# Three x loads sent one pair sooner, statistics rounded in the aggregation, the first tile in halves, the last group in two parts: a transformer block on one core

## Chip, cores and metric

The kernel runs on 1 core of one Trainium2 chip. The metric is the device time of one execution in microseconds (us). The time is the profiled span plus about 2.2 us. Before the change the median was 1081.53 us of 3 runs (1080.9 to 1082.35).

## The reference, cut to what matters

```python
h  = x + attention(layernorm(x))        # x: 2048 x 1024, 32 heads of 32, one shared K and V head
h2 = h + glu(layernorm(h))              # gate and up 1024 x 3584, down 3584 x 1024
# attention: q = x@wq; k = x@wk; v = x@wv; softmax(q k^T / sqrt(32)) v; then @ wo
# glu: (sigmoid(x@w_gate) * (x@w_up)) @ w_down
```

## The kernel before

The rows of x are 16 tiles of 128. The layer norm of tiles 0 and 1 is transposed on TensorE, that of tiles 2 to 15 by transposing transfers. At the very start TensorE runs dummy matmuls whose results nobody uses. K and V are made for two tiles at a time. Then come 512 score groups: each has 8 small row-packed matmuls on TensorE (several of them at once, on different rows of the array) and two exponentials of 128 x 1024 on ScalarE. Between them TensorE does P*V (the exponentials times V, packed by columns), q, the output projection and as much of the feed-forward part as fits; the rest of the feed-forward part stands at the end.

No order is written by hand. A list scheduler with guessed durations builds one list per engine, and the lists are then emitted with semaphores. A moved dependence therefore moves other instructions too, and the tuple `KNOBS` (one entry per eight score groups) steers the order in the middle.

```python
def op(self, eng, fn, deps=(), order=(), occ=60.0, lat=None, prio=5, key=None, nbytes=0): ...
    # (cut) "pe" goes into its list at once; the others wait in a heap until their deps have an end,
    # and the smallest (prio, seq) that is ready goes first
# ... (cut)
def load_x(ts, deps=()):
    sl = slice(ts[0] * P, (ts[-1] + 1) * P)
    o = dma(lambda: SP.dma_start(x_sb[:, ts[0]:ts[-1] + 1, :], xf[sl, :].rearrange("(a p) n -> p a n", p=P)),
            f"x{ts[0]}", P * D * 2 * len(ts), deps, prio=1 if ts[0] > 5 else 0)
# ... (cut)
def stats(ph, ts, srcs, deps, prio, small=None):
    # ... two bn_stats a and b for each tile (cut)
        c = pl.op("dve", lambda k=k, t=t: DVE.bn_aggr(mv[:, ph, t, :], st[:, k, :, :]), [a, b], prio=prio_s, ...)
    d = pl.op("dve", lambda: DVE.tensor_copy(out=mvb[:, ph, sl, :], in_=mv[:, ph, sl, :]), cs, prio=prio_s, ...)  # to bf16
    e = pl.op("dve", lambda: DVE.tensor_copy(out=mvr[:, ph, sl, :], in_=mvb[:, ph, sl, :]), [d], prio=prio_s, ...)
    # ... (cut)
for ts in [[0], [1]] + [[t, t + 1] for t in range(2, NT, 2)]:
    sv = stats(0, ts, [x_sb[:, t, :] for t in ts], [[x_ld[t]] for t in ts], ...)
    # ... centre and scale each tile on VectorE: xnorm[t] (cut)
    if 1 < ts[-1] < NT - 6:
        load_x([ts[-1] + 5, ts[-1] + 6], [xnorm[ts[-1]]])
# ... (cut)
exps[u] = pl.op("act", lambda slot=slot, pb=pb: ACT.activation(
    out=pslot(slot).rearrange("p (a b) -> p a b", a=2), in_=S_ps[:, pb:pb + 2, :],
    func=ACTF.Exp, scale=SCALE), [last] + free, prio=3, **t_act(1024))
# ... (cut)
def mk_D(t, dc):                       # down projection of a tile: 512 of 1024 columns, 28 matmuls
    def after(b, last):
        sl = slice(dc * 512, (dc + 1) * 512)
        e = pl.op("dve", lambda: DVE.scalar_tensor_tensor(
            out=h_sb[:, t % 4, sl], in0=F_ps[:, b, :], scalar=0.5, in1=h_sb[:, t % 4, sl],
            op0=ALU.mult, op1=ALU.add), [last], prio=2, **t_dve(512))
        out_dma[(t, dc)] = dma(lambda: SP.dma_start(of[t * P:(t + 1) * P, sl], h_sb[:, t % 4, sl]), ...)
```

The softmax here doesn't subtract the row's maximum and nothing guards it: scores larger than these inputs give would overflow.

## Time and profile before

| What | Before |
|---|---|
| median of the first 3 runs | 1081.53 us |
| the profiled run, time and span | 1082.78 and 1080.5 us, mean granted clock 0.998 (1 is full speed) |
| TensorE, ScalarE, VectorE busy | 97, 93, 84% |
| last exponential to last matmul | some 62 us, TensorE alone |

One row of the costliest groups is ScalarE's exponentials: count, busy us and mean ns of one, then the idle time before them and what ended it.

```profile
L693 ACT ACTIVATE Pr<-S_ps 128x1024 bf16<-128x1024 f32 x1024 | 969.2, 1179 | 4.7 <-PE S_ps L401 4.5
```

The timeline has 16 of them back to back in 14.97 us, from the first start to the last end. From one start to the next the median of the 984 between 60 and 1012 us is 0.904 us, so 1024 of them need some 926 us of a 1080 us program. A record lasts 1.179 us in the mean, so those of neighbours overlap, and a wait of up to some 0.27 us between two of them leaves no idle time in the profile; this will matter below. The Trainium skill, "ScalarE: Activation LUTs", section "What ACT_TABLE_LOAD costs", gives 186 + 0.833 N ns for such an instruction, of which about 93 ns overlap when they stand back to back: 946 ns for N = 1024, near to the 904 that the trace shows.

### The profile page before, as it was taken

The numbers are of one execution on the slowest core, as the hardware profiler recorded it, in microseconds if no ns is written. First come the engines' busy times: TensorE is split into PE (matmuls) and PEld (weight loads), VectorE is DVE, ScalarE is ACT, GpSimd is POOL, SyncE is SP. The second block draws the span as 40 slices with busy tenths as digits, with TensorE's granted clock in tenths as the row PEclk, the third lists the DMA queues.
The fourth block names the chain that finished last, engine by engine and source line by source line (L and its number), as shares of the span: only waits on it lengthen the run. The fifth ranks groups of instructions, "written<-read, shape, count | busy, mean of one in ns | idle before, by whom it ended". The sixth has DMA issues, their size and how long they took to land.

```text
span 1080.5 us, 31405 instructions
## 1 busy us (share of the span) xinstructions
PE 1045.8 (97%) x12803; PEld 483.2 (45%) x12972; DVE 902.7 (84%) x1750; ACT 1007.9 (93%) x1172; POOL 28.4 (3%) x58
## 2 busy tenths in 40 slices
PE   9999999999999999999999999999999999999998
PEld 6664444444444444444444444444444444444443
DVE  8789989898988889898888889898898989898721
ACT  6899999999999999999999999999999999999610
POOL 2100000000000000000000000000000000000000
PEclk9999999999999999999999999999999999999999
DMA  9997799927969597939659697987969596876994
GB/s 223 177 300 236 184 290 258 280 66 217 243 174 243 148 277 186 288 85 288 159 142 223 165 280 139 258 201 179 236 151 274 120 279 165 229 201 167 281 269 109
DMA packets 309359, 226.60 MB, mean 210 GB/s; under 512 B 121824, under 2 KB 300512, under 8 KB 309216
## 3 DMA queue, kind: packets, MB, share of 16 engines
q1 hardware_dynamic: 307136, 224.46, 81.3%
q8 instruction: 102, 1.67, 0.7%
q10 hardware_dynamic: 2080, 0.13, 0.1%
q14 instruction: 41, 0.34, 0.1%
HBM read 194.12 MB, written 7.86 MB: 187 GB/s over the span
## 4 chain that ended last, share of the span: by engine, by line
PE 77%; ACT 11%; DVE 5%; issue 5%; DMA 2%; SPq 0%; POOL 0%; DVEq 0%; ACTq 0%
PE F_ps L401 64%; PE S_ps L401 13%; ACT Pr L693 9%; DVE Ts L727 2%; DMA ring<-in_A_x_dram 1%; ACT tnh L968 1%; DVE st L338 1%; DVE st L340 1%; DMA zone<-ring 1%; DVE Rc L786 0%; DVE ring L385 0%; DVE hst L972 0%; DVE hact L287 0%; DVE Ts L734 0%; DVE ring L378 0%
## 5 line engine op out<-in xcount | busy, mean ns | idle before, releaser
L693 ACT ACTIVATE Pr<-S_ps 128x1024 bf16<-128x1024 f32 x1024 | 969.2, 1179 | 4.7 <-PE S_ps L401 4.5
L727 DVE TENSOR_TENSOR Ts<-Ts,Pr 128x1024 bf16<-128x1024 bf16 x736 | 482.5, 677 | 33.6 <-ACT Pr L693 31.7
L401 PE MATMUL F_ps<-ring,hnT 128*128 128x512 bf16 (+1 forms) x2005 | 411.8, 380 | 13.1 <-issue 9.6
L401 PEld LDWEIGHTS F_ps<-ring,hnT 128*128 128x128 bf16 (+1 forms) x2089 | 153.3, 97 | 192.3 <-issue 47.3
L401 PE MATMUL F_ps<-zone,hact 128*128 128x512 bf16 (+1 forms) x1153 | 212.1, 380 | 9.0 <-issue 8.2
L401 PE MATMUL S_ps<-QTb,kT 32*128 32x256 bf16 x4096 | 208.8, 273 | 1.1
L401 PEld LDWEIGHTS S_ps<-QTb,kT 32*128 32x128 bf16 x4096 | 64.1, 92 | 209.1 <-ACT Pr L693 143.5
L401 PE MATMUL F_ps<-Pr,Vb 128*32 128x256 bf16 x4096 | 135.3, 274 | 0.3 <-issue 0.3
L968 ACT ACTIVATE tnh<-F_ps 128x512 f32<-128x512 f32 x112 | 83.0, 742 | 43.1 <-PE F_ps L401 43.0
L401 PEld LDWEIGHTS F_ps<-zone,hact 128*128 128x128 bf16 (+1 forms) x1214 | 80.0, 97 | 92.7 <-issue 22.7
L727 DVE TENSOR_TENSOR Ts<-Pr 128x1024 bf16<-128x1024 bf16 x128 | 87.3, 684 | 39.9 <-ACT Pr L693 39.8
L972 DVE SCALAR_TENSOR_TENSOR hst<-tnh,F_ps 128x512 bf16<-128x512 f32 x112 | 76.6, 684 | 43.9 <-PE F_ps L401 40.8
L401 PEld LDWEIGHTS F_ps<-Pr,Vb 128*32 128x32 bf16 x4096 | 97.6, 96 | 30.2 <-issue 17.6
L401 PE MATMUL F_ps<-zone 128*128 128x256 bf16 (+5 forms) x639 | 74.9, 271 | 4.7 <-DMA zone<-ring 2.4
L401 PE MATMUL F_ps<-wo_sb,OT 128*128 128x512 bf16 (+1 forms) x289 | 61.5, 380 | 1.8 <-issue 1.4
L401 PEld LDWEIGHTS F_ps<-zone 128*128 128x128 bf16 (+1 forms) x646 | 43.6, 98 | 26.9 <-issue 7.6
L734 DVE TENSOR_TENSOR Ts<-Ts 128x1024 bf16<-128x1024 bf16 x64 | 44.0, 688 | 1.3
L1002 DVE SCALAR_TENSOR_TENSOR h_sb<-F_ps,h_sb 128x512 bf16<-128x512 f32 x32 | 21.8, 682 | 22.3 <-PE F_ps L401 22.1
L352 POOL TENSOR_SCALAR zb<-mvb 128x1 bf16<-128x1 bf16 (+1 forms) x25 | 10.3, 411 | 997.9 <-DVE mvb L348 997.9
L401 PEld LDWEIGHTS F_ps<-wo_sb,OT 128*128 128x128 bf16 (+1 forms) x304 | 22.4, 97 | 28.0 <-issue 7.0
L771 DVE COPY Oc<-F_ps 128x256 f32<-128x256 f32 x60 | 25.2, 420 | 7.4 <-PE F_ps L401 6.6
L776 DVE TENSOR_TENSOR Oc<-F_ps,Oc 128x256 f32<-128x256 f32 x60 | 25.4, 423 | 4.8 <-PE F_ps L401 3.2
(60 smaller groups left out, 333.2 us busy)
## 6 DMA issues: line engine op xcount, KB each, us to landing
ring<-in_B_w_gate_dram SPq DMA_DIRECT2D x314, 256.0 KB, 4.3
ring<-in_B_w_up_dram SPq DMA_DIRECT2D x310, 256.0 KB, 4.6
zone<-in_B_w_down_dram SPq DMA_DIRECT2D x28, 256.0 KB, 4.0
h_sb<-in_A_x_dram SPq DMA_DIRECT2D x16, 256.0 KB, 4.8
out_dram<-h_sb SPq DMA_DIRECT2D x32, 128.0 KB, 3.0
ring<-in_A_x_dram SPq DMA_DIRECT2D x7, 512.0 KB, 5.4
QTb<-q_scratch SPq DMA_DIRECT2D x14, 256.0 KB, 4.8
Pr<-in_B_w_up_dram SPq DMA_DIRECT2D x14, 256.0 KB, 4.4
```

The lines of the kernel that those rows point to most:

```text
L338: a = pl.op("dve", lambda k=k, src=src: DVE.bn_stats(st[:, k, 0, :], src[:, 0:512]), dep, prio=prio, occ=590, lat=756, order=[st_user.get(k)])
L340: b = pl.op("dve", lambda k=k, src=src: DVE.bn_stats(st[:, k, 1, :], src[:, 512:1024]), dep, prio=prio, occ=590, lat=756, order=[st_user.g ...
L352: f = pl.op("pool", lambda: POOL.tensor_scalar(out=zb[:, ph, sl].unsqueeze(2), in0=mvb[:, ph, sl, 1:2], scalar1=LN_EPS_BF16, scalar2=None, ...
L401: fn = lambda: PE.matmul(o, lhsT=l, rhs=r, start=start, stop=stop, **kw)
L693: exps[u] = pl.op("act", lambda slot=slot, pb=pb: ACT.activation(out=pslot(slot).rearrange("p (a b) -> p a b", a=2), in_=S_ps[:, pb:pb + 2 ...
L727: o = pl.op("dve", lambda T=T, a=a, b=b: DVE.tensor_tensor(out=T, in0=a, in1=b, op=ALU.add), deps, prio=4, **t_dve(1024, 1.92))
L734: merge_ev[G] = pl.op("dve", lambda T4=T4: DVE.tensor_tensor(out=T4[:, :, 0, :], in0=T4[:, :, 0, :], in1=T4[:, :, 1, :], op=ALU.add), [sum ...
L771: oc_ev[G] = pl.op("dve", lambda: DVE.tensor_copy(out=Oc[:, :], in_=O), [last, o_ev.get(G - 1)], prio=0, **t_dve(256))
L776: a = pl.op("dve", lambda: DVE.tensor_tensor(out=Oc[:, :], in0=O, in1=Ob, op=ALU.add), [last, oc_ev[G], o_ev.get(G - 1)], prio=0, **t_dve( ...
L968: tanh_of[n] = pl.op("act", lambda: ACT.activation(out=tnh[:, n % 2, :], in_=F_ps[:, b, :], func=ACTF.Tanh, scale=0.5), [last, tn_user.get ...
L972: e = pl.op("dve", lambda: DVE.scalar_tensor_tensor(out=hst[:, n % NST, :], in0=tnh[:, n % 2, :], scalar=1.0, in1=F_ps[:, b, :], op0=ALU.a ...
L1002: e = pl.op("dve", lambda: DVE.scalar_tensor_tensor(out=h_sb[:, t % 4, sl], in0=F_ps[:, b, :], scalar=0.5, in1=h_sb[:, t % 4, sl], op0=ALU ...
```

## The change

The intent: x arrives before VectorE asks for it, so that TensorE does not run dry near 43 us; the rounding copy of the statistics goes, as the aggregation writes bf16 itself; the first tile starts on its first half; the last sum and store are half as long. The settings of the scheduler were searched again for the new start. Cut: the values of `KNOBS`, a rule that may give an Oc copy (the result of P*V taken out of PSUM) to ScalarE (it never does in this program), and the use of the last new field, which may put the feed-forward sum earlier in VectorE's list.

```diff
-XT = 1000.0
+XT = 1300.0                              # the scheduler's guess for a transposing transfer
-    KNOBS = [(4, 6, 0, 0, 2), ... 65 entries ]
+    KNOBS = [(4, 7, 0, 2, 1, 0, 1), ... 65 entries, all retuned, two more fields ]
-        load_x([0])
+        x0_ld = [dma(lambda hf=hf: SP.dma_start(x_sb[:, 0, hf * 512:(hf + 1) * 512], xf[0:P, hf * 512:(hf + 1) * 512]),
+                     f"x0{hf}", P * D, (), prio=0) for hf in range(2)]
+        x_ld[0] = x0_ld[1]
...
-                c = pl.op("dve", lambda k=k, t=t: DVE.bn_aggr(mv[:, ph, t, :], st[:, k, :, :]), [a, b], prio=prio_s,
+                c = pl.op("dve", lambda k=k, t=t: DVE.bn_aggr(mvb[:, ph, t, :], st[:, k, :, :]), [a, b], prio=prio_s,
...
-            d = pl.op("dve", lambda: DVE.tensor_copy(out=mvb[:, ph, sl, :], in_=mv[:, ph, sl, :]), cs, prio=prio_s,
-                      occ=66, lat=240)
...
+                elif t == 0:
+                    for hf in range(2):
+                        xnorm[hf - 1] = pl.op("dve", lambda xh=xt[:, hf * 512:(hf + 1) * 512], sc=sc: DVE.tensor_scalar(
+                            out=xh, in0=xh, scalar1=sc, scalar2=None, op0=ALU.mult), [cen, sv[1]], prio=-1, occ=200, lat=370)
...
-            if 1 < ts[-1] < NT - 6:
-                load_x([ts[-1] + 5, ts[-1] + 6], [xnorm[ts[-1]]])
+            for k in {3: [8, 10], 5: [12], 7: [14]}.get(ts[-1], []):
+                load_x([k, k + 1], [xnorm[ts[-1]]])
...
-                    for dc in range(2):
-                        queues["D"].append(mk_D(t, dc))
+                    for a in [(0,), (1,)] if t < NT - 1 else [(0,), (1, 0, 256), (1, 256, 256)]:
+                        queues["D"].append(mk_D(t, *a))
...
-        def mk_D(t, dc):
+        def mk_D(t, dc, c0=0, n=512):     # c0 and n run through its matmuls, its sum and its store
```

More of the change, by code (lines that the diff above doesn't have):

```diff
@@ L170, in bass_sequential_preLN__grouped_kv_mqa__glu_gated_glu__prompt_kernel @@
     NCR = 12
-    KNOBS = [(4, 6, 0, 0, 2), (4, 7, 1, 0, 2), (0, 6, 0, 4, 2), (1, 5, 0, 1, 2), (4, 7, 0, 2, 2), (1, 4, 0, 4, 2), (3, 0, 1, 2, 2), (2, 7, 0, 2, 2), (3, 4, 1, 2, 3), (0, 4, 1, 4, 2), (3, 5, 0, 2, 2), (1, 7, 0, 0, 3), (3, 7, 1, 1, 3), (3, 0, 1, 4, 2), (3, 4, 0, 1, 3), (4, 4, 1, 4, 3), (3, 5, 1, 0, 2), (1, 5, 0, 4, 2), (0, 0, 0, 2, 3), (2, 5, 1, 0, 2), (1, 7, 0, 2, 3), (3, 4, 0, 2, 3), (4, 6, 0, 1, 2), (3, 0, 0, 4, 3), (4, 6, 1, 0, 3), (2, 7, 0, 2, 2), (4, 7, 0, 2, 2), (3, 7, 0, 4, 2), (4, 7, 1, 0, 3), (3, 0, 0, 2, 3), (0, 5, 0, 0, 3), (2, 5, 1, 2, 3), (2, 4, 0, 2, 2), (3, 4, 0, 2, 2), (3, 4, 0, 2, 2), (1, 4, 1, 2, 3), (4, 0, 0, 2, 2), (3, 0, 0, 2, 2), (3, 7, 0, 2, 2), (0, 4, 0, 2, 2), (1, 0, 1, 1, 2), (2, 0, 0, 4, 3), (3, 4, 0, 2, 2), (0, 7, 0, 0, 3), (2, 7, 0, 2, 2), (2, 4, 0, 4, 2), (4, 0, 0, 4, 3), (2, 4, 1, 0, 3), (4, 0, 1, 2, 2), (4, 6, 1, 2, 3), (2, 0, 0, 2, 2), (2, 6, 0, 1, 3), (2, 0, 1, 2, 2), (0, 4, 1, 4, 2), (3, 5, 0, 2, 2), (2, 7, 0, 2, 3), (0, 0, 0, 2, 2), (4, 0, 1, 4, 3), (4, 7, 0, 0, 2), (0, 5, 0, 2, 3), (4, 4, 0, 2, 2), (4, 4, 0, 2, 2), (4, 4, 0, 2, 2), (4, 4, 0, 2, 2), (4, 0, 0, 2, 2)]
+    KNOBS = [(4, 7, 0, 2, 1, 0, 1), (1, 7, 1, 2, 1, 0, 0), (3, 4, 0, 2, 3, 2, 1), (2, 0, 0, 2, 2, 2, 0), (1, 7, 0, 2, 3, 0, 1), (2, 7, 0, 2, 3, 0, 0), (0, 0, 1, 2, 2, 0, 1), (0, 0, 0, 1, 2, 0, 1), (1, 0, 0, 1, 2, 0, 0), (3, 4, 0, 1, 2, 2, 0), (3, 7, 1, 1, 2, 0, 1), (4, 0, 0, 4, 2, 2, 0), (3, 7, 0, 1, 3, 0, 0), (2, 0, 1, 4, 2, 1, 0), (3, 4, 0, 1, 2, 0, 0), (0, 4, 0, 0, 2, 0, 0), (3, 7, 0, 0, 3, 0, 1), (3, 7, 0, 2, 3, 0, 0), (0, 7, 0, 2, 3, 0, 0), (3, 5, 1, 0, 2, 0, 0), (1, 6, 0, 0, 3, 0, 0), (0, 0, 1, 1, 3, 0, 1), (1, 7, 0, 1, 3, 1, 1), (4, 6, 0, 1, 3, 0, 0), (4, 4, 1, 0, 3, 0, 0), (4, 7, 1, 1, 3, 0, 1), (2, 7, 0, 2, 2, 0, 0), (0, 5, 0, 2, 2, 0, 1), (0, 7, 1, 1, 2, 0, 1), (4, 0, 0, 4, 3, 0, 1), (0, 5, 0, 2, 3, 0, 0), (2, 0, 1, 1, 3, 1, 0), (4, 0, 0, 2, 3, 1, 0), (1, 4, 0, 1, 3, 0, 0), (3, 7, 0, 2, 2, 0, 1), (2, 4, 0, 4, 3, 0, 0), (4, 7, 0, 4, 3, 1, 0), (3, 7, 0, 2, 3, 0, 1), (3, 7, 0, 2, 2, 0, 0), (4, 0, 0, 0, 2, 0, 0), (4, 0, 1, 4, 2, 0, 0), (4, 6, 0, 2, 3, 1, 0), (1, 0, 0, 0, 2, 1, 0), (1, 7, 1, 4, 2, 1, 1), (2, 0, 0, 2, 2, 0, 1), (3, 5, 0, 0, 3, 0, 1), (1, 0, 0, 1, 2, 0, 0), (2, 5, 0, 1, 3, 0, 0), (4, 0, 0, 1, 2, 2, 1), (4, 6, 0, 2, 3, 0, 1), (2, 6, 0, 1, 2, 2, 1), (3, 0, 1, 1, 2, 2, 0), (0, 0, 1, 4, 2, 0, 0), (4, 6, 1, 1, 3, 1, 0), (0, 0, 0, 2, 3, 2, 0), (0, 7, 1, 1, 2, 0, 0), (4, 4, 0, 1, 2, 0, 1), (1, 0, 0, 4, 3, 2, 1), (4, 0, 0, 0, 2, 1, 1), (4, 5, 1, 4, 2, 0, 0), (1, 0, 0, 4, 3, 2, 0), (2, 6, 0, 2, 1, 2, 0), (4, 0, 0, 2, 2, 0, 1), (4, 4, 0, 2, 2, 0, 0), (4, 0, 0, 2, 2, 0, 0)]
@@ L211, in bass_sequential_preLN__grouped_kv_mqa__glu_gated_glu__prompt_kernel @@
         st = SB("st", [4, 2, 6], F32)
-        mv = SB("mv", [2, NT, 2], F32)
         mvb = SB("mvb", [2, NT, 2])
@@ L337, in stats @@
                 k = t % 4
-                a = pl.op("dve", lambda k=k, src=src: DVE.bn_stats(st[:, k, 0, :], src[:, 0:512]), dep, prio=prio, occ=590,
+                a = pl.op("dve", lambda k=k, src=src: DVE.bn_stats(st[:, k, 0, :], src[:, 0:512]), dep[:1], prio=prio, occ=590,
                           lat=756, order=[st_user.get(k)])
-                b = pl.op("dve", lambda k=k, src=src: DVE.bn_stats(st[:, k, 1, :], src[:, 512:1024]), dep, prio=prio,
+                b = pl.op("dve", lambda k=k, src=src: DVE.bn_stats(st[:, k, 1, :], src[:, 512:1024]), dep[-1:], prio=prio,
                           occ=590, lat=756, order=[st_user.get(k)])
-                c = pl.op("dve", lambda k=k, t=t: DVE.bn_aggr(mv[:, ph, t, :], st[:, k, :, :]), [a, b], prio=prio_s,
+                c = pl.op("dve", lambda k=k, t=t: DVE.bn_aggr(mvb[:, ph, t, :], st[:, k, :, :]), [a, b], prio=prio_s,
                           occ=120, lat=284)
@@ L347, in stats @@
             n = len(ts)
-            d = pl.op("dve", lambda: DVE.tensor_copy(out=mvb[:, ph, sl, :], in_=mv[:, ph, sl, :]), cs, prio=prio_s,
-                      occ=66, lat=240)
-            e = pl.op("dve", lambda: DVE.tensor_copy(out=mvr[:, ph, sl, :], in_=mvb[:, ph, sl, :]), [d], prio=prio_s,
+            e = pl.op("dve", lambda: DVE.tensor_copy(out=mvr[:, ph, sl, :], in_=mvb[:, ph, sl, :]), cs, prio=prio_s,
                       occ=80, lat=240)
@@ L353, in stats @@
                 out=zb[:, ph, sl].unsqueeze(2), in0=mvb[:, ph, sl, 1:2], scalar1=LN_EPS_BF16, scalar2=None, op0=ALU.add),
-                [d], prio=prio_s, occ=330, lat=440)
+                cs, prio=prio_s, occ=330, lat=440)
             hb = half if n == 1 else half.to_broadcast([P, n])
@@ L371, in bass_sequential_preLN__grouped_kv_mqa__glu_gated_glu__prompt_kernel @@
         for ts in [[0], [1]] + [[t, t + 1] for t in range(2, NT, 2)]:
-            sv = stats(0, ts, [x_sb[:, t, :] for t in ts], [[x_ld[t]] for t in ts],
+            sv = stats(0, ts, [x_sb[:, t, :] for t in ts], [[x_ld[t]] if t else x0_ld for t in ts],
                        *((3, None) if ts[0] > 1 else (3, 1) if ts[0] else (0, -1)))
@@ L445, in after @@
                 return [e]
-            gr = Group("xT", atoms, lambda: [xnorm[t], c_id], after)
+            gr = Group("xT", atoms, lambda: [xnorm[t if t or hf else -1], c_id], after)
             if t == 1:
@@ L770, in after @@
                 if h == 0:
-                    oc_ev[G] = pl.op("dve", lambda: DVE.tensor_copy(out=Oc[:, :], in_=O), [last, o_ev.get(G - 1)],
-                                     prio=0, **t_dve(256))
+                    fa, fd = both(Oc[:, :], O)
+                    if pl.free["dve"] + sum(o.occ for o in pl.heap["dve"] if o.prio < 2) > pl.free["pe"] + (1e9, 500.0, 0.0)[KNOBS[min(v, NV - 1) // WIN][5]]:
+                        oc_ev[G] = pl.op("act", fa, [last, o_ev.get(G - 1)], prio=1, **t_act(256))
+                    else:
+                        oc_ev[G] = pl.op("dve", fd, [last, o_ev.get(G - 1)], prio=0, **t_dve(256))
                     flush_sums()
@@ L989, in bass_sequential_preLN__grouped_kv_mqa__glu_gated_glu__prompt_kernel @@
         d_last = {}
-        def mk_D(t, dc):
+        def mk_D(t, dc, c0=0, n=512):
             fts = [4 * p + f for u, p in TP if u == t for f in range(4)]
             def atoms(b):
-                return [(mm(F_ps[:, b, :], hactT[:, t % 2, ft, :], wd_sb[:, ft, dc * 512:(dc + 1) * 512],
-                            ft == fts[0], ft == fts[-1]), 512, [hact_ev[(t, ft)]] if dc == 0 else []) for ft in fts]
+                return [(mm(F_ps[:, b, 0:n], hactT[:, t % 2, ft, :], wd_sb[:, ft, dc * 512 + c0:dc * 512 + c0 + n],
+                            ft == fts[0], ft == fts[-1]), n, [hact_ev[(t, ft)]] if dc == 0 else []) for ft in fts]
             def after(b, last):
-                sl = slice(dc * 512, (dc + 1) * 512)
+                sl = slice(dc * 512 + c0, dc * 512 + c0 + n)
                 d_done[t] += 1
@@ L1002, in after @@
                 e = pl.op("dve", lambda: DVE.scalar_tensor_tensor(
-                    out=h_sb[:, t % 4, sl], in0=F_ps[:, b, :], scalar=0.5, in1=h_sb[:, t % 4, sl],
-                    op0=ALU.mult, op1=ALU.add), [last], prio=2, **t_dve(512))
-                out_dma[(t, dc)] = dma(lambda: SP.dma_start(of[t * P:(t + 1) * P, sl], h_sb[:, t % 4, sl]),
-                                       f"o{t % 4}{dc}", P * 1024, [e], prio=2)
-                if (t, 1 - dc) in out_dma:
+                    out=h_sb[:, t % 4, sl], in0=F_ps[:, b, 0:n], scalar=0.5, in1=h_sb[:, t % 4, sl],
+                    op0=ALU.mult, op1=ALU.add), [last], prio=2 - KNOBS[min(v, NV - 1) // WIN][6], **t_dve(n))
+                out_dma[(t, dc + c0 / 512)] = dma(lambda: SP.dma_start(of[t * P:(t + 1) * P, sl], h_sb[:, t % 4, sl]),
+                                       f"o{t % 4}{dc}{c0 // 256}", P * 2 * n, [e], prio=2)
+                if (t, 1 - dc) in out_dma and t + 4 < NT:
                     load_xr(t + 4, [out_dma[(t, 0)], out_dma[(t, 1)]])
```

## The prediction

> **What bounds the kernel now.** I read the page first: busy shares, slices and the chain that ended last.
>
> ```profile
> PE 1045.8 (97%) x12803; PEld 483.2 (45%) x12972; DVE 902.7 (84%) x1750; ACT 1007.9 (93%) x1172; POOL 28.4 (3%) x58
> ...
> PE 77%; ACT 11%; DVE 5%; issue 5%; DMA 2%; SPq 0%; POOL 0%; DVEq 0%; ACTq 0%
> ```
>
> TensorE is busy 97% of 1080.5 us. ScalarE is as full (about 40 of every 40 us from 60 to 980 us, by the windows), but its exponentials end near 1015 us and TensorE alone works the last 65 us. If attention were faster, more feed-forward work would merely be left for the end: the amount of TensorE work, plus what TensorE loses, is the time. So I looked for TensorE's losses: the windows of the first 60 us, then the TensorE timeline there and at the end.
>
> Windows of 1 us (span; busy time and count of PE, PEld, DVE, ACT, POOL; granted clock, DMA share, GB/s):
>
> ```profile
> 41.00:42.00 1.00, 1.00 (x24) 0.90 (x25) 1.00 (x5) 1.00 (x2) 0.00 (x0) 1.00 3.73 61
> 42.00:43.00 1.00, 0.55 (x13) 0.23 (x11) 1.00 (x3) 1.00 (x2) 0.00 (x0) 1.00 0.05 5
> 43.00:44.00 1.00, 0.00 (x0) 0.00 (x0) 1.00 (x4) 1.00 (x2) 0.00 (x0) 1.00 0.84 171
> 44.00:45.00 1.00, 0.08 (x1) 0.11 (x2) 1.00 (x5) 0.57 (x1) 0.00 (x0) 1.00 1.00 267
> 45.00:46.00 1.00, 1.00 (x7) 0.78 (x7) 0.45 (x4) 0.00 (x0) 0.55 (x2) 0.63 1.02 196
> 46.00:47.00 1.00, 1.00 (x20) 0.71 (x18) 0.04 (x1) 0.00 (x0) 0.38 (x1) 0.50 0.95 185
> 47.00:48.00 1.00, 1.00 (x11) 0.42 (x11) 1.00 (x3) 0.27 (x1) 0.00 (x0) 0.50 0.77 144
> 48.00:49.00 1.00, 1.00 (x9) 0.77 (x7) 0.38 (x3) 1.00 (x2) 0.00 (x0) 0.66 0.00 0
> ```
>
> TensorE stands still from 42.5 to 44.9 us, and its clock then falls below 1.00 for four windows: 0.37 + 0.50 + 0.50 + 0.34 = 1.7 us of work lost besides the 2.4 us. ScalarE starves too (3.15 us idle before 47.73). What it waited for, by the timelines of TensorE, SyncE and VectorE:
>
> ```profile
> 44.92 2.21 PE L401 MATMUL F_ps<-zone 128*128 128x256 bf16 x25 [2.37 <-DMA zone<-ring]
> ...
> 35.23 0.58 SPq L302 DMA_DIRECT2D ring<-in_A_x_dram  x1
> 35.86 2.02 SPq L583 DMA_DIRECT2D q_scratch<-hact  x4
> 37.92 2.89 SPq L456 DMA_TRANSPOSE zone<-ring  x2
> ...
> 22.47 0.69 DVE L338 BATCH_NORM_STATS2 st<-ring 128x6 f32<-128x512 bf16 x1 [0.71 <-DMA ring<-in_A_x_dram]
> 29.18 0.69 DVE L338 BATCH_NORM_STATS2 st<-ring 128x6 f32<-128x512 bf16 x1 [0.38 <-DMA ring<-in_A_x_dram]
> 35.01 0.69 DVE L338 BATCH_NORM_STATS2 st<-ring 128x6 f32<-128x512 bf16 x1 [0.72 <-DMA ring<-in_A_x_dram]
> 39.77 0.69 DVE L338 BATCH_NORM_STATS2 st<-ring 128x6 f32<-128x512 bf16 x1 [0.77 <-DMA ring<-in_A_x_dram]
> ```
>
> The K/V projection of tiles 10 and 11 waits for their transposing transfers, issued from 37.92 and landed at 44.8; by the issue view these two took 6.1 and 5.8 us to land, against a median of 3.7, with an x load (issued 35.23) and stores of q around them. Ahead of that, VectorE, which makes the layer norm, stands four times for an x load, 2.58 us in all, though each load was sent as late as the buffer count of the code asks.
>
> The rest of the loss is structure. I took TensorE's timeline apart by kind: a 512-column matmul costs 0.215 us, a 256-column one 0.109, each change between row-packed scores, column-packed P*V and full matmuls 0.10 to 0.11, and a full matmul after scores that followed a column stretch another 0.22. In the program before there are 1042 such changes, over 100 us; the change can hardly touch them.
>
> **What the Trainium skill says.** "TensorE: Matmul & The Clock Gate", section "What's actually happening": the clock is halved after an idle window of about 3.4 us and restored after about 3.4 us of work. The trace agrees on the length (0.63 to 0.66 over 45 to 49 us), but a gap of 2.4 us was enough here. The same page, "Back-to-back issue gap", gives N/2.4 + 2.5 ns, 216 for 512 columns; 56 matmuls of the last tile took about 12.0 us, 0.215 each. "DMA: Bandwidth & Descriptors", "Latency and other measured facts", puts the fixed cost of a transfer near 2 us: the last 128 KB store landed in 1.7 us, so half the bytes cannot save half.
>
> **The change part by part.**
>
> Loads sooner. The load of tiles 10-11 now goes out with 8-9 (behind the transposes of 2-3, 17.8 us before), 12-13 after tile 5, 14-15 after tile 7: each one pair, some 5 us, earlier. VectorE's waits at 29.18, 35.01 and 39.77 go (1.87 us); that at 22.47 stays, because tiles 8-9 are asked for at the same point. Removing 7 paired casts (L348, 0.17 us each, about 0.20 with its gap) adds 1.3 us over the start. Against this the new order puts three more q evacuations (0.42 us) on VectorE before tiles 10-11 are done. For tiles 10-11: 36.7 us becomes about 36.7 - 0.4 - 0.7 (waits) - 0.7 (casts) + 1.3 = 36.2. Little; but no x load is in flight beside their transposes any more. Issued at about 37 and landing in 4 to 5 us they are there at 41 to 42.5. The K/V group that needs them stands 0.5 us further down TensorE's program (38.1 us of summed work to its end, 37.6 before) with about 5.3 us of offset ahead: needed at about 42. So I expect the gap gone or under 0.5 us, and no throttling. Tiles 12-13 and 14-15 gain 2 to 5 us and are not late. Worth 2.4 + 1.7 = 4.1 us, of which I count nine tenths, 3.7.
>
> First tile. The first transposes start at 7.27 us, after load (2.83 us), statistics, two casts and a scale of 0.49 us. Halves let the first statistics begin perhaps 0.2 us earlier, the removed cast saves 0.24, the half scale 0.24: 0.7 us. TensorE fills this time with dummy matmuls, 14 before and 12 now. Tiles 4-5 land at about 14.7 us whatever VectorE does (8.9 us after issue), so VectorE's lead is mostly lost there; TensorE keeps about 0.5 us.
>
> Schedule. Built, the program has 6 dummies fewer: two are in the first tile, four of 256 columns are 0.4 us. Changes between kinds fall from 1042 to 1037 and the dear sequence rises from 122 to 123: 5 x 0.106 - 0.22 = 0.3 us less. The new rule that may give an Oc copy to ScalarE never does: the count of Oc copies is the same on both engines. The 65 retuned settings of the windows of eight score groups only permute the middle; stalls beyond structure there are, by my subtraction, some 10 us, which the search may have moved. I credit 0.5 us.
>
> Last group. 28 matmuls of 512 columns become 56 of 256: 56 x 0.109 - 28 x 0.215 = 0.1 us more. The end of it:
>
> ```profile
> 1077.63 0.69 DVE L1002 SCALAR_TENSOR_TENSOR h_sb<-F_ps,h_sb 128x512 bf16<-128x512 f32 x1 [5.35 <-PE F_ps L401]
> 1078.35 0.33 SPq L1005 DMA_DIRECT2D out_dram<-h_sb  x1
> ```
>
> A 256-column sum takes about 0.42 (the Oc rows), 0.27 less, and a 64 KB store perhaps 0.1 less: 0.3 us net.
>
> The casts of the second layer norm (18 single ones in all, 16 of them there) lie on VectorE, 84% busy, and not on TensorE: nothing.
>
> Sum: 3.7 + 0.5 + 0.4 + 0.3 + 0.5 + 0.3 = 5.7 us, so 1081.5 - 5.7 = 1075.8 us.
>
> **Rivals.** (a) The gap only moves: the SyncE queue is in order, and the transposes of 10-11 still stand behind eight stores of q, as before; if these hold it to 38 us and landing stays at 6 us, the gap is 1 to 2 us, throttled or not: 1078 to 1080. For it: the queue's order is nearly unchanged; against it: the 512 KB load beside them is gone. (b) The two loads sent together slow each other and delay tiles 8-9 (4.6 us to landing before): VectorE then waits longer than 0.71 us at 22, and all behind shifts: 1077 to 1078. DMA share there is 0.74 in 20 to 25 us, so there is room. (c) The retuned settings remove several us of stalls in the middle, or add them: 1071 to 1073, or 1079. Nothing in the profile can tell, as only the order changes. (d) All is hidden, because ScalarE is the bound: speaks for it its 40 of 40 us; against it, its 3.15 us of starvation is in the same gap, and it is idle for the last 65 us.
>
> **Range and chances.** (a) and (b) reach up, (c) both ways; 1072.0 to 1079.5. Two per cent would be 21.6 us; TensorE's waits without structure do not add up to that, and a loss of that size would need a new wait that recurs. Faster 0.01, within 0.985, slower 0.005.
>
> **What would show it.** Right: no TensorE gap over 0.5 us between 40 and 55 us, clock 1.00 there, no VectorE wait for x after 25 us; transposes of the first tile before 6.8 us; last sum 0.42 us; windows of 40 us from 60 on shifted but as full. Wrong: a wait for zone by transfer of over 1 us anywhere before 60 us, a clock under 1 after 10 us, or a span of the middle (60 to 1015 us) that moved by over 3 us against the start.

## The result, and the profile after

The changed kernel took 1080.14 us (median of 4 runs, 1079.52 to 1080.94), the kernel before 1081.27 (median of 4). All ratios here are the mean time of one kernel's fast runs over that of the other's fast runs of the same rounds, so not quite the ratio of the medians. This one is 0.9988, with a 95% interval of 0.9971 to 1.0006: the same time. That is far above the predicted 1075.8 and outside its range.

The page of the kernel after, busy shares and chain:

```profile
PE 1067.9 (99%) x12961; PEld 486.2 (45%) x12961; DVE 901.5 (84%) x1731; ACT 1008.2 (94%) x1168; POOL 31.7 (3%) x58
...
PE 96%; DVE 1%; ACT 1%; DMA 1%; issue 1%; SPq 0%; DVEq 0%
```

TensorE seems to have become busier, 99% after 97%, but the counts say why: the trace before has 12803 matmuls and 12972 weight loads, so 169 matmul records are missing from it, and 12961 of 12961 are there now. Another, complete trace of the kernel before also has 99% and a chain with 94% TensorE. Of the 18 traces kept, the five complete ones have 99%, and 93 to 96% in the chain; the 13 that lack matmuls have 97%, and 77 to 86%. So neither the 97% nor the 77% of the chain that I had started from was a property of the kernel.

Windows of 1 us of the kernel after, columns as in the prediction (span; PE, PEld, DVE, ACT, POOL; clock, DMA share, GB/s):

```profile
42.00:43.00 1.00, 1.00 (x28) 0.66 (x26) 1.00 (x4) 1.00 (x2) 0.00 (x0) 1.00 0.86 205
43.00:44.00 1.00, 1.00 (x17) 0.82 (x10) 0.96 (x5) 1.00 (x2) 0.46 (x2) 1.00 0.42 121
44.00:45.00 1.00, 1.00 (x16) 0.59 (x13) 0.93 (x4) 1.00 (x2) 0.88 (x1) 1.00 1.04 200
45.00:46.00 1.00, 1.00 (x29) 0.90 (x22) 0.96 (x4) 0.97 (x2) 0.00 (x0) 1.00 0.93 183
```

The gap and the slow clock are gone, as predicted. Yet the time hardly moved. The timelines of TensorE and VectorE of the kernel after (start, us, the instruction, and the idle time before it with its releaser):

```profile
7.06 0.66 PE L433 MATMUL F_ps<-ident,ring 128*128 128x128 bf16 x8 [0.43 <-DVE ring L385]
10.73 0.62 PE L433 MATMUL S_ps<-ident,ring 128*128 128x128 bf16 x8 [0.59 <-DVE ring L388]
...
4.09 0.69 DVE L341 BATCH_NORM_STATS2 st<-ring 128x6 f32<-128x512 bf16 x1 [0.26 <-DMA ring<-in_A_x_dram]
9.39 0.69 DVE L339 BATCH_NORM_STATS2 st<-ring 128x6 f32<-128x512 bf16 x1 [0.56 <-DMA ring<-in_A_x_dram]
22.62 0.69 DVE L339 BATCH_NORM_STATS2 st<-ring 128x6 f32<-128x512 bf16 x1 [0.31 <-DMA ring<-in_A_x_dram]
...
1075.19 0.42 DVE L1008 SCALAR_TENSOR_TENSOR h_sb<-F_ps,h_sb 128x256 bf16<-128x256 f32 x1 [2.63 <-PE F_ps L404]
```

No wait for x after 25 us is left. The first tile started its transposes at 7.06 us, not before 6.8. Its second half made VectorE wait 0.26 us at 4.09, but a load in one piece brings them no sooner (7.11 us in a_x0whole, below). The last sum took 0.42 us.

### The profile page after: what moved, and what is told of

It reads as the page before. It is cut to its first block, busy times and chain, and to the rows that moved or that the text cites. A ratio compares the mean times of both kernels' runs of the same rounds, so it can differ in the third digit from the quotient of the medians.

```text
span 1077.7 us, 31536 instructions
## 1 busy us (share of the span) xinstructions
PE 1067.9 (99%) x12961; PEld 486.2 (45%) x12961; DVE 901.5 (84%) x1731; ACT 1008.2 (94%) x1168; POOL 31.7 (3%) x58
## 4 chain that ended last, share of the span: by engine, by line
PE 96%; DVE 1%; ACT 1%; DMA 1%; issue 1%; SPq 0%; DVEq 0%
PE F_ps L404 80%; PE S_ps L404 16%; ACT Pr L696 1%; DMA ring<-in_A_x_dram 1%; DVE Ts L730 0%; DVE Rc L786 0%; ACT QTb L285 0%; DVE hact L286 0%; SPq L316 0%; DVE Rc L797 0%; DVE OT L800 0%; DVE Rc L790 0%; DVE st L339 0%; DVE Ts L737 0%; ACT hact L285 0%
## 5 line engine op out<-in xcount | busy, mean ns | idle before, releaser
L404 PE MATMUL F_ps<-ring,hnT 128*128 128x512 bf16 (+1 forms) x2096 | 431.4, 380 | 2.2 <-issue 1.6
L404 PE MATMUL F_ps<-zone,hact 128*128 128x512 bf16 (+2 forms) x1215 | 223.0, 375 | 0.2 <-issue 0.2
L404 PEld LDWEIGHTS F_ps<-zone,hact 128*128 128x128 bf16 (+1 forms) x1215 | 83.7, 97 | 90.5 <-issue 20.9
L404 PE MATMUL F_ps<-zone 128*128 128x256 bf16 (+4 forms) x640 | 74.1, 269 | 1.4 <-DVE Rc L786 1.1
L404 PE MATMUL F_ps<-wo_sb,OT 128*128 128x512 bf16 (+1 forms) x313 | 64.5, 380 | 0.0
L1008 DVE SCALAR_TENSOR_TENSOR h_sb<-F_ps,h_sb 128x512 bf16<-128x512 f32 (+1 forms) x33 | 22.2, 671 | 22.7 <-PE F_ps L404 22.4
```

The lines of the kernel that those rows point to most:

```text
L404: fn = lambda: PE.matmul(o, lhsT=l, rhs=r, start=start, stop=stop, **kw)
L1008: e = pl.op("dve", lambda: DVE.scalar_tensor_tensor(out=h_sb[:, t % 4, sl], in0=F_ps[:, b, 0:n], scalar=0.5, in1=h_sb[:, t % 4, sl], op0=A ...
```

## The experiments

Sixteen runs were made, in four calls on three chips; every call has its own runs of the kernel before, on the same chip, and between calls only the ratios compare. Some have a mean clock of 0.998: there TensorE ran 3.4 us at half clock. I call these the dear runs. Five or six executions were timed for most, four for three of them. The frozen edits below act after the scheduler has decided all orders, so that nothing else moves.

### The kernel before, again

No edit. It asks whether the profile that I predicted from was a usual one.

> The kernel before against itself: shows the noise, and whether the lowered clock after the TensorE gap is in every run. My theory now: the gap of 2.4 us at 42 to 45 us is there each time, but the lowered clock behind it (0.998 over the whole of the profiled run) is an accident of the run, so most runs have a mean clock of 1.000, and the run that was profiled was dearer than the usual one by up to 1.7 us. Rival: the dip is in all runs, every mean clock is 0.998. Both: ratio 1.000 within 0.001.

Measured: 1081.31 us median, ratio 0.9997 (0.9984 to 1.001). Its profiled run took 1080.57 us, 2.2 us less than the one predicted from. Windows and TensorE line of this run:

```profile
42.00:43.00 1.00, 0.78 (x22) 0.43 (x18) 1.00 (x4) 1.00 (x3) 0.00 (x0) 1.00 0.52 112
43.00:44.00 1.00, 0.25 (x3) 0.25 (x4) 1.00 (x3) 1.00 (x2) 0.00 (x0) 1.00 0.90 242
44.00:45.00 1.00, 1.00 (x23) 0.93 (x21) 0.97 (x6) 0.80 (x1) 0.05 (x1) 1.00 1.12 209
...
43.75 1.54 PE L401 MATMUL F_ps<-zone 128*128 128x256 bf16 x25 [0.98 <-DVE st L338]
```

The same kernel, and a gap of 0.98 us instead of 2.37, with the clock at 1.00 throughout. In both the gap ends 0.13 to 0.14 us after the second transposing transfer for tiles 10 and 11 has landed (the view names VectorE here, but the landing fits); that transfer took 5.47 us in the first profile and 4.48 in this one. The kernel before ran 43 times: in 10 of them the mean clock was 0.998, and these averaged 1082.86 us (1082.24 to 1083.43); the other 33 averaged 1081.36 (1080.06 to 1083.19). The whole set averages 1081.71. In the six profiles with the unchanged start (these two, b_tail and the three light kernels below) the gap is 0.98 to 2.37 us. So the loss near 43 us differs from run to run, and my profile had fallen on one of the dear quarter.

### Only the loads sooner, and only the loads later

Before, with the three loads moved (frozen), and the changed kernel with them moved back (frozen):

```diff
+        sp = lists["sp"]                      # before, after the scheduler: b_early
+        # x10 right behind x8; x12 and x14 take the places of x10 and x12
+        x10.deps, x12.deps, x14.deps = [xnorm[3]], [xnorm[5]], [xnorm[7]]
```
```diff
+        sp = lists["sp"]                      # changed, after the scheduler: a_late
+        # x10 and x12 take the places of x12 and x14; x14 behind the transpose of tile 9
+        x10.deps, x12.deps, x14.deps = [xnorm[5]], [xnorm[7]], [xnorm[9]]
```

> The kernel before with only the x loads of tiles 10 to 15 sent one pair sooner; every other instruction in the place where it stood. Theory A (the loads are what removed the gap, and a gap removed early is kept to the end): no TensorE gap over 0.5 us at 40 to 46 us, time 2 to 4 us under before (ratio 0.9965 to 0.998). Theory B (the new order of TensorE's program removed it, the loads are worth nothing): the gap stays over 1.5 us, ratio 1.000. Theory C (the gap goes, but ScalarE paces the middle and gives the gain back): gap under 0.5 us, yet ratio 0.9995 to 1.000.

> The changed kernel with the x loads of tiles 10 to 15 put back to where they were sent before (place in the queue and wait), all other instructions as in the changed kernel. Theory A: a TensorE gap of over 1.5 us is back at 40 to 46 us, time 1.5 to 3 us over the changed kernel, so ratio to before 1.0005 to 1.002. Theory B: no gap, the time of the changed kernel (ratio 0.9985 to 0.999). Theory C: gap back, the time within 0.5 us of the changed kernel.

Measured: b_early 1080.58 us, 0.9991 (0.9979 to 1.0004), all clocks 1.000. a_late 1083.62 us, 1.0018 (1.0005 to 1.0031), four of six runs with a clock of 0.998. TensorE in b_early, at the start and in the tail:

```profile
43.27 1.54 PE L401 MATMUL F_ps<-zone 128*128 128x256 bf16 x25 [0.56 <-DMA zone<-ring]
...
1032.09 1.04 PE L401 MATMUL F_ps<-zone,hact 128*128 128x512 bf16 x4 [0.40 <-DMA hact<-hst]
```

TensorE and VectorE in a_late:

```profile
42.44 1.79 PE L404 MATMUL F_ps<-Pr,Vb 128*32 128x256 bf16 x32 [3.19 <-DVE mvb L343]
...
41.27 0.69 DVE L339 BATCH_NORM_STATS2 st<-ring 128x6 f32<-128x512 bf16 x1 [1.44 <-DMA ring<-in_A_x_dram]
```

The mechanism of the prediction stands: the moment at which x is loaded decides whether TensorE stands still there, and without the early loads the changed kernel stalls worse than the kernel before. In the old order they leave a gap of 0.56 us. But the 2 to 4 us of my theory A did not come: against a run of the kernel before without the slow clock there is little left to win. The last exponential of b_early starts 0.48 us earlier than that of before_again (1011.44 and 1011.92), and a tail that is 0.60 us longer, with a 0.40 us wait for a transposing transfer in it, takes that back.

### The first tile whole; the casts alone

The changed kernel with the first tile in one load (frozen), and the kernel before without the casts (frozen):

```diff
+        lists["sp"].remove(x0_ld[1])          # a_x0whole
+        x0_ld[0].fn = lambda: SP.dma_start(x_sb[:, 0, :], xf[0:P, :])
+        # every wait for x0_ld[1] becomes one for x0_ld[0]
```
```diff
-                c = pl.op("dve", lambda k=k, t=t: DVE.bn_aggr(mv[:, ph, t, :], st[:, k, :, :]), ...   # b_nocast
+                c = pl.op("dve", lambda k=k, t=t: DVE.bn_aggr(mvb[:, ph, t, :], st[:, k, :, :]), ...
+        # the 25 casts are taken off VectorE's list, and who waited for one waits for its aggregation
```

> The changed kernel with the first x tile loaded by one transfer again (the scale stays in halves, every instruction in its place). In the trace of the changed kernel the second half lands at 4.05 us and tiles 2 and 3, issued 0.47 us later, hold VectorE for 0.56 us at 9.39. If the halves are a loss: the transposes of tile 1 start about 0.4 us earlier than 10.73, and the time is 0.3 to 0.6 us under the changed kernel (ratio to before 0.998 to 0.9985). Rival, the halves are a gain or nothing: the time is equal to 0.3 us above it (0.9988 to 0.9993).

> The kernel before with only the 25 casts taken out (the aggregation writes bf16), every other instruction in its place. VectorE reaches tiles 10 and 11 some 0.7 us sooner, but then waits longer for the x loads, which go out late as before. Expected: equal to before, ratio 0.999 to 1.0005, slow kind of run still there. Rival, VectorE's time is on the path of the start and the gap shrinks: 0.5 to 1 us less.

Measured: a_x0whole 1079.68 us, 0.9984 (0.9972 to 0.9996), no slower than the changed kernel, which has 0.9982 to 0.9988 in the calls in which it ran; its first score group starts at 12.81 us, that of another run of the changed kernel at 12.82. No gain of the halves can be seen. b_nocast 1081.41 us, 1.0002 (0.999 to 1.0015), two of five runs at the slow clock; in its profile TensorE stands 2.08 us at the same place and VectorE waits 2.16 us for x at 39.93 us. The time that the casts took, VectorE waits for x instead. No gain of their removal can be seen either.

### The settings of the middle

The changed kernel again, and with the old settings from the 33rd score group on:

```diff
+KNOBS = new[:4] + [old + (0, 0) for old in before[4:]]      # a_oldknobs
```

> The changed kernel once more, as the mark for the others of this call. The traces so far say: the kernel before has two kinds of run, near 1080.6 us and near 1082.7 us (the clock falls to half for 3.4 us at 45 us in the second kind), the changed kernel only one kind. Expected 1079.5 to 1080.5 us with all mean clocks 1.000, 0.5 to 1 us under the good kind of before. Rival: it has slow kinds of its own, up to 1082.

> The changed kernel with the old settings from the 33rd score group on (81 us); the start is equal to the last instruction. In the traces the changed kernel stands 1.3 us ahead of the good kind of before at the 20th group, and only 0.2 us ahead at the last. If the retuned settings gave that back (1.1 us lost): 0.5 to 1.5 us under the changed kernel. Rival, the settings are tuned to this start and their loss of old ones is worse: 1 to 4 us over the changed kernel. The ScalarE trace should show no idle after 60 us if the first holds; the changed kernel has 0.8 us there, the kernel before none.

Measured: after_again 1080.05 us, 0.9982 (0.9969 to 0.9995); a_oldknobs 1081.0 us, 0.9995 (0.9982 to 1.0007), on the same chip. My theory that the new settings had given the gain back fell: on this start they are worth about 0.9 us by the medians (1.4 by the means), though the intervals overlap. The traces show what they move. From the 61st exponential to the last the kernel before takes 932.9 us, a_oldknobs 933.8 and the changed kernel 935.2; but after the last exponential has started the changed kernel needs 63.8 us and the other two 66.3. It has 403 matmuls left there (counted by their weight loads), a_oldknobs 420. So the new settings do more of the feed-forward part beside the exponentials and leave less of it for the end.

### ScalarE or TensorE as the bound of the attention part

The kernel before with 32 exponentials of half the columns, with 88 feed-forward matmuls of half the columns, and with both. Their outputs are wrong, which doesn't matter for the times.

```diff
+                k = 1 if v >= 64 and v % 14 == 0 and i else 2          # b_light_act: ScalarE 32 x 0.427 = 13.7 us less
-                    out=pslot(slot)...[:, 0:2, :], in_=S_ps[:, pb:pb + 2, :],
+                    out=pslot(slot)...[:, 0:k, :], in_=S_ps[:, pb:pb + k, :],
```
```diff
+                    n = FW // 2 if 2 <= t <= 12 and p % 2 == 0 and dt == 4 else FW   # b_light_pe: TensorE 88 x 0.107 = 9.4 us less
-                    r.append((mm(F_ps[:, b, :], ..., piece(sl[d])[:, dt % DPP, :], ...
+                    r.append((mm(F_ps[:, b, 0:n], ..., piece(sl[d])[:, dt % DPP, 0:n], ...
```

> Wrong results on purpose. The kernel before, 32 of its 1024 exponentials, spread evenly from the 64th group on, work on half their columns (about 0.43 us less each, 13.7 us of ScalarE work); every instruction keeps its place. My prediction held that the amount of TensorE work is the time and ScalarE's fullness costs nothing: then the time falls by less than 2 us. Theory now, ScalarE paces TensorE through the attention part (it never idles from 60 to 1012 us, and TensorE waits a little at most score groups, some 15 us in all): the last exponential comes 8 to 13 us sooner and so does the end.

> Wrong results on purpose. The kernel before, 88 of the feed-forward matmuls inside the attention part (tiles 2 to 12) at 256 columns instead of 512, 88 x 0.107 = 9.4 us less TensorE work; every instruction keeps its place. The prediction's step (TensorE's work is the time): the end comes 9 us sooner. Theory now (ScalarE paces this part): the last exponential and the end come at most 2 us sooner, as TensorE only waits longer.

> Wrong results on purpose. The kernel before with both cuts at once: 32 exponentials at half width (13.7 us less on ScalarE) and 88 feed-forward matmuls at half width (9.4 us less on TensorE). Alone, the first made the good run 0.5 to 1 us shorter, the second not at all. If the two engines are equally full through the attention part, each cut having turned into waits of the engine that was cut, both together should bring the end 5 to 10 us sooner. Rival, a third thing sets that part (VectorE, the transfers, or the length of the round from scores to exponential and back): less than 3 us sooner.

Measured: b_light_act 1080.24 us, 0.9985 (0.9971 to 0.9999). b_light_pe 1081.89 us, 1.0 (0.9985 to 1.0015). b_light_both 1076.66 us, 0.9957 (0.9943 to 0.997). Nine microseconds of TensorE work alone bought nothing, fourteen of ScalarE alone one to two, far from the 8 to 13 that I had expected; both together bought four to five. That is a little under the range that I had set for it, and above the rival's. The traces say the same without the luck of the start: from the start of the 61st exponential to that of the last it takes 932.9 us in before and in before_again, 931.1 in b_light_act, 932.8 in b_light_pe and 928.1 in b_light_both. One window of each over the attention part; before_again first, then b_light_act and b_light_pe (TensorE's pair cannot be compared, as the last two traces lack matmuls):

```profile
60.00:1012.00 952.00, 948.79 (x11724) 414.25 (x11726) 837.26 (x1590) 952.00 (x1088) 17.63 (x30) 1.00 0.81 210
```
```profile
60.00:1012.00 952.00, 925.44 (x11593) 413.94 (x11755) 836.86 (x1593) 946.40 (x1089) 17.59 (x30) 1.00 0.80 210
```
```profile
60.00:1012.00 952.00, 925.08 (x11552) 419.78 (x11715) 837.07 (x1590) 952.00 (x1087) 17.58 (x30) 1.00 0.80 210
```

ScalarE (the fourth pair) was busy 952 of 952 us, and with 13.7 us of work less it is busy 5.6 us less. So a share of 1.00 is not the whole truth about an engine: some of that time is waiting that the records show as busy. By my estimate from the overlap of the records, up to 0.27 us can hide behind each of the 32 cut exponentials, 8.6 us, which covers the missing 8.1 (13.7 less 5.6). The code shows how the two engines are tied: the score matmuls of a group wait for exponentials of the two groups before, as three pairs of PSUM banks hold the scores. A cut on one engine alone turned almost wholly into its waiting; neither is the bound alone. What holds the rest of the 9.4 us that b_light_both could have won is not shown.

### The last group, from both sides, and the two useful parts together

The changed kernel with the last group whole (twice), the kernel before with the split alone, and the kernel before with the early loads and the split and nothing else (twice):

```diff
-                    for a in [(0,), (1,)] if t < NT - 1 else [(0,), (1, 0, 256), (1, 256, 256)]:     # a_nosplit, a_nosplit_2
+                    for a in [(0,), (1,)]:
```
```diff
+                    for a in [(0,), (1,)] if t < NT - 1 else [(0,), (1, 0, 256), (1, 256, 256)]:     # b_tail: mk_D as in the change;
-                    for dc in range(2):                                  # b_early_tail, b_early_tail_2: and the moves of b_early
```

The third call:

> The changed kernel with the last group whole again (one product of 512 columns, one sum, one store of 128 KB); all before it is equal to the last instruction. The predicted term was 0.3 us net; by the traces the time from the last matmul to the end fell from 2.96 to 2.5 us and 0.1 us of matmul was added. Expected: 0.3 to 0.4 us slower than the changed kernel (1080.1 to 1080.4). Rival, the store's landing is as long as before: no difference.

> The kernel before with two parts of the change alone, nothing else moved: the early x loads and the split last group. If these two carry what the change gains and the other parts (halves of the first tile, casts, retuned settings) cancel each other: 1080.0 to 1080.4 us, all clocks 1.000, that is within 0.4 us of the changed kernel. Rival, the other parts carry some: 0.5 us or more over the changed kernel.

The fourth call, where all four stand side by side:

> The changed kernel once more. My theory: 1080.0 us (1079.4 to 1080.5), all clocks 1.000, and within 0.5 us of b_early_tail_2 in this call. Rival (the rest of the change is worth something): 0.5 to 1.5 us faster than b_early_tail_2.

> The kernel before with the x loads sooner and the last group split, nothing else. My theory: 1079.7 us, all clocks 1.000, ratio 0.998 to 0.999. Rival: 1080.5 to 1081.2.

> The kernel before with only the last group split; no earlier instruction moves on any engine. My theory: 0.3 to 0.5 us faster than before in runs of the same kind, and both kinds of run are still there: some near 1080.2 with clock 1.000, some near 1082.3 with clock 0.998. Rival, that the split is worth 1 us: good runs at 1079.6. In the trace the last matmul still ends near 1075.3 or 1077.6 us, and the span ends 2.5 us after it instead of 2.96.

> The changed kernel with the last group whole, once more, now beside the changed kernel on the same chip. My theory: 0.3 to 0.5 us slower than after_third (1080.3 to 1080.5), the 1.1 us of the first time having been the chip and one run with K/V waits. Rival: 1.0 us slower again.

| Kernel | median us | runs | ratio to before (95%) |
|---|---|---|---|
| a_nosplit | 1081.14 | 5 | 0.9996 (0.9982 to 1.001) |
| b_early_tail | 1079.7 | 5 | 0.9984 (0.9972 to 0.9997) |
| after_third | 1079.8 | 5 | 0.9986 (0.9974 to 0.9999) |
| b_early_tail_2 | 1079.85 | 5 | 0.9985 (0.9971 to 0.9998) |
| b_tail | 1081.41 | 5 | 1.0002 (0.9989 to 1.0014) |
| a_nosplit_2 | 1080.52 | 5 | 0.9992 (0.998 to 1.0005) |

First: the kernel before with two of the parts is as fast as the whole change on the same chip, 1079.85 and 1079.8 us. Second: the split alone, b_tail, keeps the dear runs, two of five, at 1082.41 and 1083.04 us with a clock of 0.998. Its TensorE and VectorE lines in such a run:

```profile
44.36 1.59 PE L401 MATMUL F_ps<-zone 128*128 128x256 bf16 x25 [1.63 <-DMA zone<-ring]
...
1077.69 0.42 DVE L1002 SCALAR_TENSOR_TENSOR h_sb<-F_ps,h_sb 128x256 bf16<-128x256 f32 x1 [2.63 <-PE F_ps L401]
```

From the last matmul to the end of the span it takes 2.5 us (1077.65 to 1080.14), where the kernel before took 2.9 (1077.59 to 1080.52): 0.43 less. Against this the halved matmuls take a little longer. In b_early_tail, whose tail has no new wait, it takes 65.97 us from the start of the last exponential to the end, in before and before_again 66.34: 0.37 us net. The times are noisier than this: the good runs of b_tail average 1081.10 us beside 1081.31 for the good runs of before of that call, 0.2 us, and its median missed my expectation of 1080.2; a_nosplit_2 is 0.7 us over after_third by medians, and a_nosplit was 1.1 us over another call's changed kernel. I take 0.37 us, which the traces show, for the split; the 1.1 us of the first time I do not hold, since the profiled run of a_nosplit, 1083.27 us, had other waits, which lie a thousand microseconds before the edit:

```profile
44.48 1.03 PE L404 MATMUL F_ps<-zone 128*128 128x256 bf16 x8 [0.84 <-DMA zone<-ring]
55.28 1.40 PE L404 MATMUL F_ps<-zone 128*128 128x256 bf16 x23 [1.54 <-DMA zone<-ring]
```

So the changed kernel's start can stall too, on the transposing transfers, in one of the seven profiles of it and of its variants that keep the early loads.

## Why the prediction was wrong

**Step 1, "Worth 2.4 + 1.7 = 4.1 us, of which I count nine tenths, 3.7": mis-sized; this is the step that made the number wrong.** The removal of the gap was right, the size was not. Early loads were worth 1.0 us in the first call (b_early averages 1080.83, before 1081.87) and 1.85 in the fourth (b_early_tail_2 1079.90, b_tail 1081.75, two of five of them dear). Three errors lie in the term. I read the loss in a profiled run of 1082.78 us and subtracted it from a median of 1081.53: 1.25 us of the 5.7 was never in the number that I subtracted from. I took one run for the kernel, although this gap varies between its runs, from 0.98 to 2.37 us. And the slow clock cost 1.1 us, not 1.7. What TensorE did after the late K/V group (scores, projections, P*V) shows it, in before and then in before_again:

```profile
47.06 0.61 PE L401 MATMUL S_ps<-QTb,kT 32*128 32x256 bf16 x8
47.61 1.77 PE L401 MATMUL F_ps<-zone 128*128 128x256 bf16 x10
49.64 1.06 PE L401 MATMUL F_ps<-Pr,Vb 128*32 128x256 bf16 x32
...
45.23 0.40 PE L401 MATMUL S_ps<-QTb,kT 32*128 32x256 bf16 x8
45.56 1.56 PE L401 MATMUL F_ps<-zone 128*128 128x256 bf16 x10
47.38 1.06 PE L401 MATMUL F_ps<-Pr,Vb 128*32 128x256 bf16 x32
```

From the start of the late K/V group (44.92 and 43.75, shown above) to the first P*V matmul TensorE took 4.72 us in the dear run and 3.63 in the other: 1.09 us for the 3.4 us at half clock. So even in the dear run the term was 2.37 + 1.09 = 3.5 us.

**Step 2, "the amount of TensorE work, plus what TensorE loses, is the time": right for what TensorE loses in the start, wrong for its work in the attention part.** The two profiles of the kernel before test the first half. The dear one lost 1.39 us more in the gap and 1.09 by the clock; it had been 0.23 ahead before that, and from there to the end of the attention part and on to the last matmul everything comes 2.25 us later. The spans differ by as much (1080.5 and 1078.3). A loss in the start is paid in full. The second half fails by b_light_pe: 9.4 us of TensorE work less there, and the end comes no sooner.

What differs by nearly the same 2.2 us between the two profiles is also what ScalarE got done in the first 60 us. Windows of the kernel before, then of before_again (ScalarE is the fourth pair):

```profile
0.00:60.00 60.00, 55.47 (x833) 38.92 (x835) 45.26 (x125) 46.63 (x73) 9.97 (x26) 0.97 0.92 206
```
```profile
0.00:60.00 60.00, 55.71 (x858) 39.53 (x858) 47.34 (x129) 48.78 (x76) 10.09 (x26) 1.00 0.95 222
```

And of a_late, then of the kernel after:

```profile
0.00:60.00 60.00, 52.43 (x811) 38.05 (x812) 43.80 (x117) 43.53 (x66) 10.06 (x26) 0.97 0.89 204
```
```profile
0.00:60.00 60.00, 56.36 (x912) 40.77 (x912) 47.65 (x126) 48.65 (x72) 9.97 (x26) 1.00 0.97 223
```

| Profile | ScalarE busy, 0 to 60 us | span | sum |
|---|---|---|---|
| before | 46.63 | 1080.5 | 1127.1 |
| before_again | 48.78 | 1078.3 | 1127.1 |
| b_nocast | 46.71 | 1080.5 | 1127.2 |
| b_early | 49.27 | 1078.4 | 1127.7 |
| b_tail | 47.01 | 1080.1 | 1127.1 |
| b_early_tail, _2 | 49.38, 49.35 | 1077.3, 1077.7 | 1126.7, 1127.1 |
| after, _again, _third | 48.65, 49.25, 48.85 | 1077.7, 1077.5, 1077.5 | 1126.4, 1126.8, 1126.4 |
| a_late | 43.53 | 1082.9 | 1126.4 |

ScalarE's work in the first 60 us differs by 5.9 us over these, the sum by 1.3, and the right-result variants not listed lie between 1126.3 and 1127.6. What ScalarE gets done early, the span is shorter by, nearly one for one. This does not single out ScalarE. In the kernels with the old order TensorE's weight loads are shifted against before_again by just as much as the exponentials from 60 us to the last exponential, so TensorE's progress would give the same table; and the light kernels show that neither engine sets the pace alone. No run slowed ScalarE's start alone. Between the two orders the sum even hides two shifts: the last exponential of the kernel after starts later than that of before_again (1013.82 and 1011.92), and its tail is 2.5 us shorter. What the table does show is how little a good run had left to lose: the three profiles of the changed kernel stand at the 61st exponential 0.4 to 1.0 us ahead of before_again, and 2.6 to 3.2 ahead of before. Most of what the change could win was what the dear runs had lost.

My rival (d), that all is hidden because ScalarE is the bound, was half right: for the 950 us between, where neither the gap nor the idle last 65 us says anything, b_light_pe shows that TensorE work saved alone is worth nothing. But b_light_act shows nearly the same for ScalarE work, and the gap in the start was not hidden.

**Step 3, first tile 0.5, dummies 0.4, schedule 0.3, settings 0.5: nothing in sum.** Since b_early_tail_2 and after_third are equal (means of 1079.90 and 1080.08 us), all else in the change adds up to zero within the noise of five runs each. Some of the first tile's saving does reach the first score group, which starts at 13.42, 12.82 and 12.91 us in the three profiles of the changed kernel and at 13.48 and 13.70 in those of the kernel before. But at the 11th exponential the changed kernel is no longer ahead of before_again (0.02 to 0.62 us later): in the new order TensorE waits for ScalarE's copies of q at 17.39, 18.58 and 21.30 us, 0.74 us in all in the kernel after, where before waits 0.13. That fewer dummies only lengthen such waits is argued, not shown; the changes between kinds are TensorE work in the attention part, where step 2 fails. The new settings are better than the old ones on the new start (0.9 us), but the old ones on the old start reach the same time: they were tuned to where they stood. And the "dear sequence" of 0.22 us does not exist. From the last score matmul to the next full one it takes 0.426 us after a column stretch in the trace before, and 0.200 without one (medians); in the complete trace of before_again it takes 0.200 in both cases. Missing matmul records had looked like lost time.

**Step 4, last group, 0.3 us net: right**, 0.37 by the traces, within the noise by the times.

**What held:** no gap over 0.5 us in 40 to 55 us, a clock of 1.00, no late wait for x, the last sum of 0.42 us, no Oc copy on ScalarE, and rival (b) false (VectorE's wait at 22.62 us is 0.31, not longer than the 0.71 of before).

**The sum.** Over all calls the changed kernel averages 1080.06 us in 14 runs, the kernel before 1081.71 in 43: 1.65 us, of which about 1.3 are the loads (the difference left for them) and 0.37 the split. Predicted were 5.7: the loads were set 2.4 too high, the rest of the start and middle 1.7. My range reached up to 1079.5, and rival (a) alone, at 1078 to 1080, reached past that; with four terms that all had the same sign, and one profile of one run beneath them, it was too narrow. What the change does buy is steadiness: no run of its 14 had a slow clock, and they span 1.6 us, against 3.4 for the kernel before. This comes from the loads: of all runs with right results and a clock on record, none of 50 with the early loads was dear, and 18 of 59 with the late ones.

**What stays open:** what makes the transposing transfers near 40 us take longer in some runs than in others. In all seven profiles with late loads and the old order the gap ends 0.13 to 0.14 us after the second of them has landed; VectorE's waits for x do not follow the gap (in all 1.49 us from 34 to 41 us before the gap of 2.37, but 1.94 before the 1.68 of b_light_pe). No run varied the memory's load by itself.

## What to carry to other kernels

Profile the kernel before more than once before sizing a stall, and subtract a loss only from the time of the run in which it was read. Where two engines are both full, take a little work from each alone and then from both: this tells in three runs whether a saving on one of them can reach the end. What a lowered clock cost is read from when the next work is done, not from the clock's share: 1.09 us here, not 1.7. And before an engine's busy share is compared, compare its counts: matmuls that were not recorded look like idle time.

## What the Trainium skill lacked or had wrong

- "TensorE: Matmul & The Clock Gate", section "What's actually happening": the clock is said to halve after at least one idle window of about 3.4 us, in windows that run free of the kernel. The length agrees: 3.4 us at half clock in the kernel before. But gaps of 1.63 us (b_tail) and 2.08 us (b_nocast) were followed by it, while one of 0.98 us was not, nor one of 1.68 us in b_light_pe; TensorE never stood still for a whole window. Other stalls, 0.84 and 1.54 us in a_nosplit, left the clock at 1.000. In 10 of 43 runs of the same kernel the clock fell, which a window that runs free would allow for, but no run here shows its phase.
- "TensorEngine Tiling (Array Packing)", section "Key Properties": it says that changing the tiling mode drains the engine, without a cost. Here each change between row-packed, column-packed and full matmuls costs 0.10 to 0.11 us, and with 1042 of them that is over 100 of 1080 us.
- "ScalarE: Activation LUTs": its figure for an instruction is near (0.904 us from start to start for 1024 columns, 0.946 by the page). No page has that a ScalarE at 952 busy us of 952 may give up 13.7 us of work and be only 5.6 us less busy, as b_light_act was.
- No page warns that a trace may lack matmul records. Here 13 of 18 do, and 169 of 12972 missing go with 97% busy instead of 99%, and with a chain of 77% TensorE instead of 94%.
